# Dividing the loads of V by partitions instead of by head pairs, in a kernel of linear attention and a token-mixing MLP

## The chip, the cores and the metric

The kernel runs on one core of one Trainium2 chip. A core has TensorE (PE, with the weight loads PEld beside it), VectorE (DVE), ScalarE (ACT), GpSimd (POOL), SyncE (SP), which here issues all transfers, and 16 DMA engines. The metric is the device time of one execution in microseconds (us), of which the median over several runs is taken.

## The reference, cut to what matters

```python
# q, k, v: (8, 8, 576, 64) f32 = batch, heads, positions, head dim
c, s = cos(pi/2 * pos/S), sin(pi/2 * pos/S)
phi = lambda x: concat([relu(x)*c, relu(x)*s], -1)
kv  = einsum('bhsf,bhsd->bhfd', phi(k), v)
z   = sum(phi(k), over s)
attn = einsum('bhsf,bhfd->bhsd', phi(q), kv) / (einsum('bhsf,bhf->bhs', phi(q), z) + 1e-6)
x = attn as (8, 576, 512)
W = einsum('bsd,btd->bst', x @ w_q, x @ w_k) / 8        # w_q, w_k: (512, 64)
out = relu(einsum('bst,btd->bsd', W, x)) @ w_out        # w_out: (512, 512)
```

## The kernel before

Work is cut into 16 units, H = 0 to 15: batch H // 2, and two of its four pairs of heads. Of each of k, q and v a unit has a raw tile of 128 partitions x 2 head pairs x 576 floats (a pair's data, 2 x 576 x 64 numbers, is read as 128 rows of 576, one to a partition: a row is 2304 contiguous bytes in DRAM). There are four raw buffers for each of k, q and v (`NRAW`), taken in turn by H % 4.

The order of all work is written out by hand in ORDER (L24 to L60); a word is a step, its unit, a place in PSUM after the colon and an engine after the @ (A is ACT, V is DVE, G is POOL). Each engine does its words strictly in this order, SyncE too, which has the loads LK, LQ, LV, the weight loads LW and the stores ST in its queue. The steps that matter here:

- LV, LK, LQ (`load`, L129): a unit's raw tile comes in by two transfers of 128 partitions, one for each head pair (L132). Only for H = 0 the halves are words of their own (LV0a, LV0b and so on).
- CV (L208, cast at L193 or L195): v to bf16, over both halves, on POOL (one half on ACT). VS (L213, DVE) multiplies it by the cos and sin table.
- RK, RQ (L187 on ACT, L189 on POOL): relu of k and q to bf16.
- KV (L234): 36 matmuls of phi(k) with v; KE (L193, L197) copies the sums out of PSUM. QT (L245): transposes of q; QM (L253, DVE) multiplies by the table.
- N (L269), EP (L277, L279), X (L286, L287): numerator, denominator and their quotient, into the tile x.
- XT or XR (L300, L313) and XE: x transposed. WK (L333), WQ (L346), KX (L360), MX (L383), ME (L394, L396), WO (L403): the token mixing as (x w_k)^T x first, then times x w_q, relu, times w_out. KW, QW, XK, XA, XB are its copies between (L193, L195, L197).
- OE (L193, L197) copies an output tile of 128 rows out of PSUM, ST (L413) stores it. LW (L417 to L421) are the three weight loads.

In all SyncE issues 135 transfers: 32 for each of k, q and v, 36 stores and 3 of weights. They take eight completion semaphores in turn, and before a transfer is issued the one that had its semaphore before it, eight transfers earlier, must have landed. A load also waits until the raw buffer's last reader (RK, RQ or CV of H - 4) is done, a store until its OE is done.

Of the kernel before, what the change touches and what calls it, by code (L numbers as in the profile page):

```python
# [63 lines left out]
def kernel(  # L64
# [10 lines left out]
    nc = tc.nc  # L75
# [4 lines left out]
    P = 128  # L80
# [12 lines left out]

    NRAW, NPREP, NV2, NQM, NX, NXT, NOUT = (4, 2, 2, 2, 2, 2, 12)
    XC = DM // 2

    pool = ctx.enter_context(tc.tile_pool(name="sb", bufs=1))
    psum = ctx.enter_context(tc.tile_pool(name="ps", bufs=1, space=bass.MemoryType.PSUM))
# [2 lines left out]
    def bufs(n, shape, dtype, name):  # L101
        return [pool.tile(shape, dtype, name=f"{name}{i}") for i in range(n)]

    raw = {nm: bufs(NRAW, [P, 2, HC], FP32, f"{nm}raw") for nm in "kqv"}
# [10 lines left out]
    wq_b = bufs(2, [P, HS], BF16, "wq")  # L115
    kx_b = bufs(2, [P, 2, XC], BF16, "kx")
    mix_b = bufs(2, [P, NDM, 2 * S], BF16, "mix")
# [5 lines left out]
    def srcs(src):  # L123
        return [src[b].flatten().rearrange("(pr p e) -> p pr e", pr=NPAIR, p=P)
                for b in range(B)]

    src = {"k": srcs(k), "q": srcs(q), "v": srcs(v)}

    def load(nm, H, part):  # L129
        b, h = divmod(H, 2)  # L130
        for r in (0, 1) if part is None else (part,):
            nc.sync.dma_start(raw[nm][H % NRAW][:, r, :], src[nm][b][:, 2 * h + r, :])  # L132

# [57 lines left out]
    def cast(eng, dst, s):  # L191
        if eng is A:
            A.copy(dst, s)  # L193
        elif eng is G:
            G.tensor_scalar(dst, s, 1.0, 1.0, op0=ALU.mult, op1=ALU.mult)  # L195
        else:
            V.tensor_copy(dst, s)  # L197
# [127 lines left out]
    def bank(i):  # L325
        return PS[:, i, :].bitcast(FP32)
# [28 lines left out]
    def KX(b, ps, eng):  # L355
        place["KX", b] = ps
        o = bank(ps)
        for u in range(SC):
            for t in range(2):
                nc.tensor.matmul(  # L360
                    o[H2 * t:H2 * t + H2, 0:XC], wk_b[b % 2][:, u, :],
                    x_b[b % NX][:, u].rearrange("p h d -> p (h d)")[:, t * XC:(t + 1) * XC],
                    start=(u == 0), stop=(u == SC - 1))

    def XK(b, ps, eng):
        cast(eng, kx_b[b % 2][:, 0, :], bank(place["KX", b])[:, 0:XC])

# [66 lines left out]
    for word in ORDER.split():  # L434
        word, _, eng = word.partition("@")
        word, _, ps = word.partition(":")
        part = {"a": 0, "b": 1}.get(word[-1])
        word = word.rstrip("ab")
        kind = word[:2] if word[:2] in steps or word[0] in "LRCVT" else word[0]
        i, ps = int(word[len(kind):] or 0), int(ps or 0)  # L440
        if kind in ("LK", "LQ", "LV"):
            load(kind[1].lower(), i, part)
        elif kind in halves:
            halves[kind](i, ps, ENG.get(eng), slice(0, 2) if part is None else
                         slice(part, part + 1))
        else:
            steps[kind](i, ps, ENG.get(eng))
# [30 lines left out]
```

## Time and profile before

| what | value |
|---|---|
| three runs | 126.8, 122.39, 124.22 us; median 124.22 |
| the profiled execution | 122.49 us |
| its span, first to last instruction | 120.7 us |
| granted TensorE clock | 0.991 |
| PE, DVE, ACT, POOL busy | 94.8, 88.2, 84.2, 52.2 us |
| packets of the transfers' queue | 20592, 39.07 MB, 89.8% of 16 engines' span |
| a V load, issue to landing, median | 6.0 us |

Busy time is that of an engine's own instructions; waits, branches and the issuing of transfers are not counted. A DMA share is the sum of the packets' times over 16 engines' time; packets overlap a little in an engine, so it can be somewhat above 1. In a list of instructions in order of time a line has the start, the time from the first start to the last end of what was merged, the engine and the line of the code, the tiles, the count, and in brackets the idle time ahead of it and what ended that. SPq is SyncE issuing a transfer. The chain is followed back from the last instruction, at each step to what released it.

### The profile page before, as it was taken

The page shows a single profiled execution, that of the slowest core. Times are in us where ns is not written, and L with a number is a line of the kernel's source. Part 1 is how long each engine was busy: PE and PEld are TensorE (multiplying, and loading weights), DVE is VectorE, ACT ScalarE, POOL GpSimd, SP SyncE. Part 2 cuts the span into 40 slices and gives each one's busy share as a digit, 9 for nine tenths or more (in the row PEclk, how much of TensorE's full clock was granted, in tenths as well). Part 3 has the DMA queues.
Part 4 walks back from the last instruction along what each step waited for, and adds up shares of the span by engine and source line. Part 5 has one row for each costly group of instructions (what it writes and reads, how often), then busy time and mean ns, then how long its engine had stood idle before and what let it go on. Part 6 is the DMA issues. An engine that isn't in the chain of part 4 may idle for free.

```text
span 120.7 us, 5301 instructions
## 1 busy us (share of the span) xinstructions
PE 94.8 (79%) x2286; PEld 63.1 (52%) x2286; DVE 88.2 (73%) x132; ACT 84.2 (70%) x155; POOL 52.2 (43%) x63
## 2 busy tenths in 40 slices
PE   0005919758778899969999999798999999999950
PEld 0004818637656656635667576454755864653410
DVE  0136998889989998997979987759969868766200
ACT  7246452967887989777967897586678668757450
POOL 2577136032739758146799304937365310010000
PEclk9999999999999999999999999999999999999996
DMA  3999999999999999999989999999997681875685
GB/s 111 318 384 405 395 391 391 361 405 396 392 390 408 398 337 344 355 360 379 383 282 326 364 285 391 343 331 283 391 299 263 238 329 55 320 288 198 237 331 196
DMA packets 20615, 39.40 MB, mean 326 GB/s; under 512 B 3184, under 2 KB 3184, under 8 KB 20592
## 3 DMA queue, kind: packets, MB, share of 16 engines
q1 hardware_dynamic: 20592, 39.07, 89.8%
q8 instruction: 18, 0.29, 1.0%
q14 instruction: 5, 0.04, 0.1%
HBM read 29.62 MB, written 9.44 MB: 324 GB/s over the span
## 4 chain that ended last, share of the span: by engine, by line
DMA 39%; PE 39%; DVE 6%; issue 4%; SPq 3%; ACT 3%; POOL 2%; DVEq 0%; ACTq 0%; POOLq 0%
DMA kraw<-in_k_dram 24%; PE ps L403 20%; DMA vraw<-in_v_dram 11%; DMA out_dram<-o 5%; PE ps L234 3%; PE ps L383 3%; PE ps L269 3%; SPq L132 3%; PE ps L360 3%; DVE v L213 2%; PE ps L313 2%; DVE x L287 2%; PE ps L245 2%; PE ps L333 2%; PE ps L346 2%
## 5 line engine op out<-in xcount | busy, mean ns | idle before, releaser
L403 PE MATMUL ps<-wow,mix 128*128 128x512 bf16 x144 | 34.7, 380 | 0.0
L287 DVE TENSOR_TENSOR x<-ps,rec 128x640 bf16<-128x640 f32 x32 | 26.4, 824 | 2.2
L195 POOL TENSOR_SCALAR vb<-vraw 128x1152 bf16<-128x1152 f32 (+1 forms) x16 | 17.9, 1122 | 20.9 <-DMA vraw<-in_v_dram 18.6
L213 DVE TENSOR_TENSOR v<-vb,vtab 128x2304 bf16<-128x2304 bf16 (+1 forms) x17 | 21.7, 1289 | 6.6 <-POOL vb L195 6.6
L253 DVE TENSOR_TENSOR qm<-ps,qtab 128x2304 bf16<-128x2304 bf16 x16 | 21.4, 1350 | 4.6 <-ACT qtab L166 2.9
L193 ACT COPY o<-ps 128x512 f32<-128x512 f32 x30 | 17.5, 587 | 6.6 <-PE ps L403 4.5
L269 PE MATMUL ps<-kvs,qm 64*128 64x65 bf16 x640 | 15.3, 199 | 6.0 <-ACT kvs L193 3.3
L403 PEld LDWEIGHTS <-mix 128*128 128x128 bf16 x144 | 12.4, 98 | 14.2 <-issue 0.9
L394 ACT ACTIVATE mix<-ps 128x576 bf16<-128x576 f32 x26 | 16.4, 657 | 3.2 <-PE ps L383 3.2
L189 POOL TENSOR_SCALAR rq<-qraw 128x1152 bf16<-128x1152 f32 x9 | 13.4, 1487 | 11.4 <-DMA qraw<-in_q_dram 10.8
L269 PEld LDWEIGHTS <-qm 64*128 64x128 bf16 x640 | 13.3, 100 | 9.4 <-issue 5.7
L189 POOL TENSOR_SCALAR rk<-kraw 128x1152 bf16<-128x1152 f32 (+1 forms) x12 | 13.8, 1150 | 9.4 <-DMA kraw<-in_k_dram 7.0
L193 ACT COPY xT<-ps 128x1280 bf16<-128x1280 bf16 (+1 forms) x13 | 15.4, 1186 | 3.3 <-PE ps L313 1.7
L234 PE MATMUL ps<-v,rk 64*64 64x130 bf16 x576 | 12.5, 236 | 3.0 <-DVE x L287 1.3
L245 PE MATMUL ps<-ident,rq 64*128 64x64 bf16 x288 | 7.6, 199 | 9.3 <-ACT rq L187 8.8
L187 ACT ACTIVATE rq<-qraw 128x1152 bf16<-128x1152 f32 (+1 forms) x8 | 8.4, 1046 | 6.6 <-DMA qraw<-in_q_dram 6.6
L234 PEld LDWEIGHTS <-rk 64*64 64x64 bf16 x576 | 10.1, 117 | 5.2 <-ACT rk L187 1.4
L245 PEld LDWEIGHTS <-rq 64*128 64x128 bf16 x288 | 6.1, 101 | 11.7 <-ACT rq L187 9.0
L383 PE MATMUL ps<-wq,kx 64*128 64x288 bf16 x64 | 8.3, 287 | 0.3 <-ACT xT L193 0.2
L195 POOL TENSOR_SCALAR kx<-kx 64x256 bf16<-64x256 bf16 x7 | 2.8, 399 | 12.6 <-ACT kx L193 12.2
L286 DVE RECIPROCAL rec<-rec 128x10 f32<-128x10 f32 x32 | 6.8, 211 | 1.8 <-ACT rec L277 1.4
L277 ACT ACTIVATE rec<-ps,eps 128x10 f32<-128x10 f32 x23 | 6.2, 273 | 1.7 <-PE ps L269 1.6
(46 smaller groups left out, 99.3 us busy)
## 6 DMA issues: line engine op xcount, KB each, us to landing
vraw<-in_v_dram SPq DMA_DIRECT2D x32, 288.0 KB, 6.0
qraw<-in_q_dram SPq DMA_DIRECT2D x32, 288.0 KB, 5.9
kraw<-in_k_dram SPq DMA_DIRECT2D x32, 288.0 KB, 5.9
out_dram<-o SPq DMA_DIRECT2D x36, 256.0 KB, 3.1
wof<-in_moe_w_out_dram SPq DMA_DIRECT2D x1, 1024.0 KB, 7.6
wqf<-in_moe_w_q_dram SPq DMA_DIRECT2D x1, 128.0 KB, 5.5
wkf<-in_moe_w_k_dram SPq DMA_DIRECT2D x1, 128.0 KB, 5.2
```

What stands on the lines that cost most here:

```text
L189: eng.tensor_scalar(dst, s, FMAX, 0.0, op0=ALU.min, op1=ALU.max)
L193: A.copy(dst, s)
L195: G.tensor_scalar(dst, s, 1.0, 1.0, op0=ALU.mult, op1=ALU.mult)
L213: V.tensor_mul(v2_b[H % NV2][:, part, :, :, 0:D], vb_b[H % NPREP][:, part].unsqueeze(3).to_broadcast([P, n, C, 2, D]), vtab.unsqueeze(1).t ...
L234: nc.tensor.matmul(kv_v[o, r, :], rk_b[H % NPREP][a, pr, c, :], v2_b[H % NV2][a, pr, c, :, 0:D + 1], start=(c == 0), stop=(c == C - 1))
L245: nc.tensor.transpose(qt_v[:, r, c * H2:(c + 1) * H2], rq_b[H % NPREP][a, c, :, :], ident[a, a])
L253: V.tensor_mul(qm_b[H % NQM][:, :, :, 0:C, :].rearrange("p s r c d -> p s r (c d)"), qt_view(place["QT", H]).unsqueeze(1).to_broadcast([P, ...
L269: nc.tensor.matmul(nv[:, pr, u, :], qm_b[H % NQM][a, s, r, 2 * u:2 * u + 2, :], kv_b[H % 2][a, r, s, 0:D + 1], start=(u == 0 and s == 0), ...
L287: V.tensor_tensor(x_b[b % NX][:, :, 4 * h:4 * h + 4, :].rearrange("p u (w r) d -> p r w u d", r=2)[:, r], nv[:, :, :, 0:D], rec.to_broadca ...
L383: nc.tensor.matmul(pair(ps)[:, t, :].bitcast(FP32)[:, 0:HS], kx_b[b % 2][a, (m // 2) ^ t, (m % 2) * P:(m % 2 + 1) * P], wq_b[b % 2][a, :], ...
L394: A.activation(dst, s, AF.Relu, scale=scale_moe)
L403: nc.tensor.matmul(o, mix_b[bp % 2][:, m, rt * P:(rt + 1) * P], wow[:, m, :], start=(m == 0), stop=(m == NDM - 1))
```

## The change

A whole load of V (all but those of H = 0) still has two transfers, and they still fill the same tile from the same addresses. But the tile is divided between them by partitions: the first transfer takes the first m partitions, of both head pairs, the second one the other 128 - m. m goes through 120, 104, 88 and 72 with H % 4. K and Q are loaded as before.

```diff
     NRAW, NPREP, NV2, NQM, NX, NXT, NOUT = (4, 2, 2, 2, 2, 2, 12)
     XC = DM // 2
+    PM = (120, 104, 88, 72)
...
     def load(nm, H, part):
         b, h = divmod(H, 2)
+        if nm == "v" and part is None:
+            m = PM[H % 4]
+            for p in (slice(0, m), slice(m, P)):
+                nc.sync.dma_start(raw[nm][H % NRAW][p], src[nm][b][p, 2 * h:2 * h + 2, :])
+            return
         for r in (0, 1) if part is None else (part,):
             nc.sync.dma_start(raw[nm][H % NRAW][:, r, :], src[nm][b][:, 2 * h + r, :])
```

The lines of the code from L96 on stand one further down in the changed kernel, those from L134 on six: L195 is L201 there, L234 is L240.

## The prediction

> **What bounds the kernel now.** I read the page's forty slices first, then the busy time by stretches, SyncE's issues in order of time, the chain that ended last, and last the two engines on which the final load is used. The slices:
>
> ```profile
> PE   0005919758778899969999999798999999999950
> DMA  3999999999999999999989999999997681875685
> GB/s 111 318 384 405 395 391 391 361 405 396 392 390 408 398 337 344 355 360 379 383 282 326 364 285 391 343 331 283 391 299 263 238 329 55 320 288 198 237 331 196
> ```
>
> A slice is 3 us. The 16 DMA engines are busy from the second slice to the 30th; TensorE is full in most slices only from the 15th on. Four stretches, with the busy time of PE, PEld, DVE, ACT and POOL, the granted clock, the DMA share and GB/s:
>
> ```profile
> 3.00:33.00 30.00, 16.57 (x516) 14.45 (x517) 22.11 (x35) 17.78 (x31) 13.61 (x20) 1.00 1.05 384
> 33.00:62.00 29.00, 26.04 (x723) 17.59 (x720) 25.92 (x36) 24.29 (x49) 18.56 (x17) 1.00 1.02 370
> 62.00:92.00 30.00, 27.86 (x703) 17.88 (x696) 24.73 (x39) 22.37 (x44) 16.05 (x16) 1.00 0.98 334
> 92.00:121.00 29.00, 24.30 (x362) 13.21 (x360) 15.45 (x25) 17.47 (x33) 3.36 (x5) 0.96 0.63 235
> ```
>
> Until 33 us only the DMA is full; from 33 to 92 us DMA and TensorE are both nearly full; after 92 us the loads are over. The last row also tells what kind of limit the DMA has: at a share of 0.63 the engines move 235 GB/s, 373 for a full share, and in the first row 384/1.05 = 366. An engine does not get faster when others rest, so each has its own rate. That rate is in SyncE's issues (start, us, line, transfer):
>
> ```profile
> 12.25 1.08 SPq L132 DMA_DIRECT2D vraw<-in_v_dram  x2
> 13.76 1.08 SPq L132 DMA_DIRECT2D kraw<-in_k_dram  x2
> 15.26 1.08 SPq L132 DMA_DIRECT2D qraw<-in_q_dram  x2
> ```
>
> Here an issue waits for the landing of the transfer eight before it, so two transfers land per 1.50 us, one per 0.75. A transfer is 128 rows of 2304 bytes (576 floats), 8 for each of 16 engines: a row costs an engine 0.75/8 = 0.094 us. That each uses all 16 is in the packet counts: 3184 packets are under 512 bytes, 1024 of them rows of the two small weight loads (2 x 128 x 4), which leaves 2160 = 135 transfers x 16, one small packet for each engine of each transfer. The chain:
>
> ```profile
> 8.25 6.24 DMA vraw<-in_v_dram
> ...
> 14.51 6.51 DMA kraw<-in_k_dram
> ...
> 21.04 5.22 DMA kraw<-in_k_dram
> ...
> 26.28 6.51 DMA vraw<-in_v_dram
> ...
> 64.38 4.83 DMA kraw<-in_k_dram
> ...
> 69.22 7.16 DMA kraw<-in_k_dram
> ...
> 110.17 6.17 PE ps L403 x28
> ```
>
> One transfer releases the next until 32.8 us; the load that lands at 76.38 is on it again; the end is TensorE's. And where the last K load is used:
>
> ```profile
> 91.91 2.26 POOL L189 TENSOR_SCALAR rk<-kraw 128x1152 bf16<-128x1152 f32 x2 [2.23 <-DMA kraw<-in_k_dram]
> ```
> ```profile
> 93.69 0.75 PE L333 MATMUL ps<-wkw,xT 128*128 128x64 bf16 x20
> 94.36 1.25 PE L234 MATMUL ps<-v,rk 64*64 64x130 bf16 x72
> ```
>
> POOL idles 2.23 us for it, ends the two casts at 94.17, and TensorE starts the 72 matmuls on them at 94.36. The load stream sets the time almost to its last load.
>
> **The change, part by part.** *Removed and added.* For 15 of the 16 values of H (H = 0 is loaded in halves and stays) two V transfers of 128 rows become two of 2m and 256 - 2m rows, m = 120, 104, 88, 72. Bytes, rows of 2304, the number of transfers (135) and SyncE's order stay. Issues cost 0.33 to 0.43 us of SyncE each, at most 135 x 0.43 = 58 us of 120.7, so issue time has room; bounds for the new shapes: 0 and, at the longest step between issues inside a pair, 15 x 2 x 0.1 = 3 us, spread over a queue that waits for landings anyway. I take 0; if that cover went, it would be those 3 us at most. CV already waited for both transfers: no wait is added or removed there.
>
> *Moved: which engine carries which row.* No row of this trace shows a transfer of another count than 128, so I bound it. Lower end: 256 rows on 16 engines evenly, as now, 0 us. Upper end of an uneven spread: a transfer takes as many engines as divide its partitions into equal whole shares, always the same first ones. 128 into 16 shares of 8 is what is seen; 120, 104 and 88 give 15, 13 and 11 shares of 8, 72 gives 12 of 6; the rests give 8 of 1, 12 of 2, 10 of 4, 14 of 4. Two rows a partition, the first eight engines then carry 16+2 = 18, 16+4 = 20, 16+8 = 24 and 12+8 = 20 rows for a V load, where they carried 16; the last engine carries none. I take this end: the shares seen are equal and whole, and equal shares of 8 are what the new counts allow.
>
> [...]
>
> Extra rows on the busiest engines: H = 4, 8, 12 give 3 x 2, H = 1, 5, 9, 13 give 4 x 4, H = 2, 6, 10, 14 give 4 x 8, H = 3, 7, 11, 15 give 4 x 4: 70 rows x 0.094 = 6.6 us. By stage, in the order of the loads: 26 rows, 2.4 us, to V4, on which the chain leaves the DMA at 32.78; 48 rows, 4.5 us, to K9 (used at 58); 58 rows, 5.4 us, to K12 (landed at 76.38, used at 76.49); 70 rows, 6.6 us, to K15.
>
> *What of it is on the path.* Until 33 us all. From 33 to 62 TensorE has 3 us of idle time in 29 and waits on little, so a part is covered there; but the stretch to 92 is entered late, and K12 and K15 are used 0.11 and 0.15 us after they land. Behind a late K load on POOL, in order, stand the other casts and the small copies of L195; behind a late V or K on SyncE all later loads and stores, each waiting for the landing eight before; TensorE waits for rk at L234 with WO, MX and N queued behind. At the end the slack is small: K15's cast ends at 93.06, K14's behind it on POOL at 94.17, and the second half of the 72 matmuls starts at 94.36 + 0.6 = 95.0: 0.8 us. After that come 22 us of TensorE work in order that cannot be moved ahead. The end moves by 6.6 - 0.8 = 5.8 us.
>
> *Sum.* The profiled execution took 122.49 us, 120.7 its span and 1.8 around it. 122.49 + 5.8 = 128.3. The median of the three runs, 124.22, is 1.7 above the profiled execution; a median to be measured again has that too: 130.0 us.
>
> **The rivals.** *A: rows get slower as well.* A row costs 0.094 us when a transfer is laid out over all 128 partitions. With other shares two engines may write into the same part of the memory at a time and halve each other. Bounds for the big piece's 16 rows: unchanged, 0, or doubled, 15 x 16 x 0.094 = 22.6 us. For: 0.094 is met by all engines at once only in that one layout. Against: engines are not in step, so a clash lasts for a part of a piece. At a third to a half of the upper bound it adds 7.5 to 11.3 us: 137.5 to 141.3.
>
> [...]
>
> *B: the gaps take the rows; not slower.* Loads do not move at the full rate throughout: 384 GB/s to 33 us, 370 to 62, 334 to 92. Against the first that is 29 x 14/384 + 30 x 50/384 = 1.1 + 3.9 = 5.0 us in which the stream stands or waits for one late engine. If these gaps belong to engines that now carry less, or to SyncE waiting (11.4 us for ACT's o at L413, not all of it felt), the rows fill them: 5.8 - 5.0 = 0.8, 125.0 us. It decides only if nearly all gaps lie so; against it, gaps that come from a release which itself waits for a load move along with that load.
>
> *C: the spread is even.* Rows are dealt out evenly whatever the count, the change then does nothing to the stream: 124.2 us. Against it, only the shares above.
>
> *D: faster.* The lightly loaded engines bring their part of every Q and K earlier, but a transfer counts as landed with its slowest engine. I see no term; 122 or less.
>
> **How the numbers follow.** The forecast 0.43, A 0.28, B 0.12, C 0.13, D 0.04. The time is the forecast's, 130.0; its own range, with 4 to 7 us added, is 128.2 to 131.2. The range reaches over B to A's upper price: 125.0 to 141.5; C, D and A's upper tail, 0.2, lie outside. About 2% (121.7 to 126.7) is what a measurement of this kernel tells from no change. Same: C 0.13 and most of B, 0.09: 0.22. Slower: the forecast, A and the rest of B: 0.74. Faster: 0.04.
>
> **What the changed profile would show.** The packet counts settle the spread: by equal shares the small packets of the 15 loads fall from 32 to 23, 25, 21 and 26 each, 3 x 9 + 4 x 7 + 4 x 11 + 4 x 6 = 123 fewer, 3184 to 3061 under 512 bytes. An even spread leaves 3184. The DMA share from 3 to 33 us falls below 1.0 and GB/s by 8 to 9%; by A more. Between a V pair and the next, SyncE's issues stand more than 1.5 us apart. The last two casts of kraw on POOL start near 98.5 instead of 91.91, and the 72 matmuls of L234 near 100; the time after them is unchanged, 26 us. If the share of DMA stays at 1.05, the forecast's step on the engines is wrong; if the packets fall to 3061 and the casts still start near 92, the gaps took it; if they start after 102, rows got slower.

## The result and the profile after

The changed kernel takes 153.41 us (median of four, 150.78 to 154.61) against 124.97 before: 28.4 us more, a ratio of 1.2292, 95% interval 1.1815 to 1.2768. 130.0 was forecast, 141.5 was the upper end of the range. Some executions of every kernel fall into a slower state, so this ratio (151.56 against 123.31 us, 28.3 more) and every time, difference and ratio of the experiments below are taken from the other executions alone, while a median is over all. The profiled execution took 150.78 us, its span is 149.0. Its slices, now of 3.7 us each:

```profile
PE   0017347257984488399759998956399999999990
DMA  4999999999999998989999899998779958467785
GB/s 116 283 393 317 273 274 256 245 305 284 212 268 339 271 216 193 226 200 217 294 353 271 260 257 312 230 346 270 167 253 343 362 195 323 181 227 266 276 295 208
DMA packets 20492, 39.40 MB, mean 264 GB/s; under 512 B 3061, under 2 KB 3061, under 8 KB 20469
q1 hardware_dynamic: 20469, 39.07, 89.3%
```

Two things are to be seen. The small packets are 3061, to the packet what equal whole shares on 15, 13, 11, 12 and on 8, 12, 10, 14 engines give: in the number of engines the spread is the one that was forecast. And the DMA digits are still nines, with 200 to 350 GB/s under them where there were 340 to 400. Stretches of the changed kernel (PE, PEld, DVE, ACT, POOL, granted clock, DMA share, GB/s):

```profile
3.00:33.00 30.00, 12.19 (x356) 10.58 (x356) 16.07 (x22) 12.44 (x23) 10.78 (x17) 0.85 1.03 292
33.00:62.00 29.00, 19.35 (x424) 14.08 (x428) 20.58 (x29) 16.09 (x28) 10.46 (x11) 0.74 0.99 256
62.00:92.00 30.00, 26.52 (x606) 17.16 (x603) 19.93 (x30) 19.08 (x38) 15.30 (x13) 0.84 0.97 264
92.00:121.00 29.00, 23.76 (x553) 15.07 (x552) 18.30 (x29) 17.91 (x35) 14.13 (x12) 0.88 0.93 289
```

For a full share the first stretch moves 292/1.03 = 283 GB/s; before it was 384/1.05 = 366. The share is a sum of packet times, so packets take longer for the same bytes. The queue line says how much: 89.3% of 149.0 us are 133.1 us per engine, 89.8% of 120.7 were 108.4, so 24.7 us more packet time for each of 16 engines. Rows that are only dealt out unevenly would have left that sum as it was (e4_rows and f2_twice below show it row by row: 102.1 and 104.4 ns in the mean against 101.7). The chain, its four V loads:

```profile
9.07 8.28 DMA vraw<-in_v_dram
...
33.73 11.18 DMA vraw<-in_v_dram
...
47.93 13.73 DMA vraw<-in_v_dram
...
62.05 11.87 DMA vraw<-in_v_dram
```

A V load, 6.2 to 6.5 us on the chain before, is now 8 to 14, and the DMA holds the chain almost without a break to 74 us instead of 33 (in the kernel before two K loads are on it once more, from 64 to 76 us). SyncE's issues of the changed kernel, each pair let go by earlier landings:

```profile
12.82 1.38 SPq L135 DMA_DIRECT2D vraw<-in_v_dram  x2
15.75 1.96 SPq L138 DMA_DIRECT2D kraw<-in_k_dram  x2
17.92 1.85 SPq L138 DMA_DIRECT2D qraw<-in_q_dram  x2
```

The pairs stand 2.9 and 2.2 us apart where 1.5 was the rule. And the end, the last two casts of K on POOL:

```profile
120.41 2.58 POOL L195 TENSOR_SCALAR rk<-kraw 128x1152 bf16<-128x1152 f32 x2 [2.06 <-DMA kraw<-in_k_dram]
```

They start at 120.41, not near 98.5 as forecast; 28.6 us remain after that, as 28.8 did before. All of the loss lies ahead of these casts.

### The profile page after: what moved, and what is told of

Read it like the earlier page. It is cut to its first block, busy times and chain, and to the rows that moved or that the text cites. A ratio compares the mean times of both kernels' runs of the same rounds, so it can differ in the third digit from the quotient of the medians.

```text
span 149.0 us, 5301 instructions
## 1 busy us (share of the span) xinstructions
PE 105.9 (71%) x2286; PEld 70.0 (47%) x2286; DVE 90.2 (61%) x132; ACT 85.0 (57%) x155; POOL 54.5 (37%) x63
## 2 busy tenths in 40 slices
DMA packets 20492, 39.40 MB, mean 264 GB/s; under 512 B 3061, under 2 KB 3061, under 8 KB 20469
## 3 DMA queue, kind: packets, MB, share of 16 engines
q1 hardware_dynamic: 20469, 39.07, 89.3%
## 4 chain that ended last, share of the span: by engine, by line
DMA 51%; PE 38%; POOL 3%; SPq 3%; ACT 2%; issue 1%; ACTq 0%; POOLq 0%
DMA vraw<-in_v_dram 30%; PE ps L409 19%; DMA kraw<-in_k_dram 15%; DMA out_dram<-o 5%; PE ps L275 3%; PE ps L389 3%; PE ps L240 3%; PE ps L251 2%; PE ps L339 2%; PE ps L319 2%; PE ps L352 2%; PE ps L366 2%; POOL vb L201 2%; SPq L138 1%; SPq L135 1%
## 5 line engine op out<-in xcount | busy, mean ns | idle before, releaser
L409 PE MATMUL ps<-wow,mix 128*128 128x512 bf16 x144 | 37.5, 403 | 0.0
L201 POOL TENSOR_SCALAR vb<-vraw 128x1152 bf16<-128x1152 f32 (+1 forms) x16 | 18.4, 1153 | 45.1 <-DMA vraw<-in_v_dram 44.1
L275 PE MATMUL ps<-kvs,qm 64*128 64x65 bf16 x640 | 15.7, 203 | 11.5 <-DVE qm L259 5.3
L240 PE MATMUL ps<-v,rk 64*64 64x130 bf16 x576 | 14.7, 261 | 9.7 <-POOL rk L195 4.4
L400 ACT ACTIVATE mix<-ps 128x576 bf16<-128x576 f32 x26 | 16.3, 654 | 8.6 <-PE ps L389 8.6
L195 POOL TENSOR_SCALAR rk<-kraw 128x1152 bf16<-128x1152 f32 (+1 forms) x12 | 14.6, 1217 | 11.4 <-DMA kraw<-in_k_dram 8.0
L240 PEld LDWEIGHTS <-rk 64*64 64x64 bf16 x576 | 12.0, 134 | 12.3 <-POOL rk L195 5.4
L251 PE MATMUL ps<-ident,rq 64*128 64x64 bf16 x288 | 9.0, 215 | 11.6 <-ACT rq L193 10.6
L195 POOL TENSOR_SCALAR rq<-qraw 128x1152 bf16<-128x1152 f32 x9 | 13.1, 1460 | 9.1 <-DMA qraw<-in_q_dram 8.1
L251 PEld LDWEIGHTS <-rq 64*128 64x128 bf16 x288 | 7.2, 110 | 16.7 <-ACT rq L193 10.7
L389 PE MATMUL ps<-wq,kx 64*128 64x288 bf16 x64 | 9.5, 310 | 3.5 <-ACT o L199 2.3
L193 ACT ACTIVATE rk<-kraw 128x1152 bf16<-128x1152 f32 (+1 forms) x5 | 5.3, 1067 | 8.6 <-DMA kraw<-in_k_dram 5.8
L201 POOL TENSOR_SCALAR kx<-kx 64x256 bf16<-64x256 bf16 x7 | 4.0, 567 | 12.5 <-ACT kx L199 12.1
L199 ACT CAST kvs<-ps 128x260 bf16<-128x260 f32 x12 | 4.5, 381 | 7.0 <-PE ps L240 7.0
```

The costliest lines, as they stand in the source:

```text
L195: eng.tensor_scalar(dst, s, FMAX, 0.0, op0=ALU.min, op1=ALU.max)
L240: nc.tensor.matmul(kv_v[o, r, :], rk_b[H % NPREP][a, pr, c, :], v2_b[H % NV2][a, pr, c, :, 0:D + 1], start=(c == 0), stop=(c == C - 1))
L251: nc.tensor.transpose(qt_v[:, r, c * H2:(c + 1) * H2], rq_b[H % NPREP][a, c, :, :], ident[a, a])
L275: nc.tensor.matmul(nv[:, pr, u, :], qm_b[H % NQM][a, s, r, 2 * u:2 * u + 2, :], kv_b[H % 2][a, r, s, 0:D + 1], start=(u == 0 and s == 0), ...
L389: nc.tensor.matmul(pair(ps)[:, t, :].bitcast(FP32)[:, 0:HS], kx_b[b % 2][a, (m // 2) ^ t, (m % 2) * P:(m % 2 + 1) * P], wq_b[b % 2][a, :], ...
L400: A.activation(dst, s, AF.Relu, scale=scale_moe)
```

## The experiments

Theory I: only the uneven counts of rows per engine cost. Theory S: rows get slower because engines write into the same part of the memory. Theory N: the order in which DRAM is read, or two head pairs in one transfer, is slow. Theory C, from the g runs on, is a form of S: how crowded the fullest part of the memory is in a transfer decides. S and C are suppositions of the author: no trace names the engine of a packet or the part of the memory that it writes, only times can speak for them. Times are means; in brackets is the difference to the mean of the kernel before, measured on the same chip beside it (122.85 for the e runs, 123.16 for f, 122.78 for g, 123.78 for h, 122.44 for i), then the ratio with its 95% interval. e2_64, e3_96, g_120, g_88 and h2_near rest on one execution each and h4_pairs on two, so they have no interval. The expectations were written from medians (12.1 us for f2_twice, for example), which differ by up to 4 us.

**e1_whole.**
```diff
-            for p in (slice(0, m), slice(m, P)): ...
+            nc.sync.dma_start(raw[nm][H % NRAW], src[nm][b][:, 2 * h:2 * h + 2, :])
```


> Each whole V load is one transfer of 128 partitions with both head pairs, so the rows of the two pairs alternate as in the changed kernel, but the partitions are dealt out as before the change. Theory S (rows got slower because engines that share a piece write into the same part of the memory) and theory I (only the uneven counts of rows per engine): both expect no loss, 122 to 126 us. Theory N (the alternating order of the rows in DRAM, or rows of two pairs in one transfer, is what is slow): 140 to 153 us.

126.85 us (+4.0; ratio 1.0325, 1.0176 to 1.0475). N falls: reading two pairs in turn costs a few us at most, not 28. The few were not followed up.

**e2_64 and e3_96.** m = 64, and m = 96, for every H.

> Each whole V load is divided 64 + 64: if the number of engines is the largest up to 16 that divides the partitions, every engine has 8 rows of each transfer, as before the change, and under 512 bytes stay 3184 packets. Theory I: no loss, 122 to 127 us. [...] Theory N: 140 to 153 us.

> Each whole V load is divided 96 + 32, again 16 engines and even counts, 12 + 4 rows for each. Theory I: no loss, 122 to 127 us. Theory S: the 4 rows of the piece of 32 cost up to double, 15 x 4 x 0.094 = 5.6 us, the 12 of the piece of 96 anything from nothing to double, 16.9 us: 129 to 147 us. Theory N: 140 to 153 us.

143.67 us (+20.8) and 140.05 (+17.2). By equal shares nothing is uneven here (both have 3184 small packets, as before the change) and most of the loss is there: I cannot be the main cause. e3_96 is in S's range, and +20.8 for e2_64 is near the 15 x 16 x 0.094 = 22.6 us that doubled rows of V would cost.

**e4_rows, f2_twice.** The loads of before, and a further transfer (two in f2_twice) for each whole V load:
```diff
+            n = (2, 4, 8, 4)[H % 4]
+            nc.sync.dma_start(scr[H % 4:32:4, 0:n, :], vrows[b][n][0:8])
```


> The loads are those before the change; beside each whole V load stands a third transfer of 2, 4, 8 or 4 further rows (with H % 4) for each of 8 engines, into an unused tile, on partitions 0, 4, 8 to 28 (shifted by H % 4), which are taken to be those that the same 8 engines write anyway: the uneven counts of the forecast (70 rows more on the busiest engines) without any sharing. 1.3 MB more are loaded. The forecast's own price, 70 x 0.094 = 6.6 less 0.8: theory I and theory S as the larger of two parts both expect 128 to 132 us. If 124 to 126, the gaps took the rows and the loss of the change is all from slower rows; if above 134, uneven counts cost more than the rows that they add.

> e4_rows with the extra rows twice (two transfers for each V load, 140 rows more on the busiest engines, again every fourth partition). It prices the forecast's step by itself: 140 x 0.094 = 13.2 less 0.8 gives 12.4 us over the kernel before, 134 to 139 us. If the gaps in the stream take the rows (rival B), 126 to 130 us.

126.86 us (+4.0; ratio 1.0326, 1.0182 to 1.0469, where 5.8 us would be 1.047) and 136.80 (+13.6; 1.1096, 1.0977 to 1.1216). Twice the rows cost about what 140 x 0.094 - 0.8 = 12.4 said. The single dose lies under its price; some rows may be taken by gaps, but the doubled dose excludes that gaps swallow them all. 4 to 7 us, from the single dose to half of the double one, is a fair price for the change's 70 rows. It includes whatever the 15 or 30 further transfers cost in themselves.

**f1_near, f4_pairs.** e4_rows with other partitions, meant for the same 8 engines:
```diff
-            nc.sync.dma_start(scr[H % 4:32:4, 0:n, :], vrows[b][n][0:8])
+            nc.sync.dma_start(scr[8 * (H % 4):8 * (H % 4) + 8, 0:n, :], vrows[b][n][0:8])  # f1_near
+            nc.sync.dma_start(scr[H % 4:64:8, 0:n, :], vrows[b][n][0:8])                   # f4_pairs
```


> As e4_rows, the same 70 extra rows on the same 8 engines in the same transfers, but written to 8 neighbouring partitions (8 x (H % 4) and the 7 after it) in place of every fourth. Theory I (only the count of rows per engine matters): as e4_rows, 126 to 129 us. Theory S (engines that write into the same part of the memory halve each other): if 4 engines share each of two such parts, a row costs up to 4 x 0.094, 70 x 0.38 = 26.3 less 0.8: 135 to 151 us.

> [...] Theory I: 126 to 129 us. Theory S: a row up to double, 70 x 0.188 = 13.2 less 0.8, so between e4_rows and 138 us, and below f1_near.

138.15 us (+15.0; 1.1217, 1.1130 to 1.1304) and 132.28 (+9.1; 1.0740, 1.0543 to 1.0938). Same bytes, same source rows and the same number of engines as e4_rows' +4.0 (3304 small packets in all three, 8 for each further transfer); only the partitions written differ. That the eight engines are the same ones is assumed, no count shows it. The order, neighbours worst (+15.0), then every eighth (+9.1), then every fourth (+4.0), is the one in which theory S had priced them.

**f3_evenodd.** e2_64 with `(slice(0, P, 2), slice(1, P, 2))`.

> V divided 64 + 64 as in e2_64, but into even and odd partitions, so that each transfer reaches all of the memory and each engine has the same 8 rows of it. Theory I: as before the change, 123 to 127 us. Theory S as the number of parts reached (64 neighbours reach half of them): 123 to 128 us. [...]

124.71 us (+1.6; 1.0126, 1.0049 to 1.0203). Its stretches:

```profile
3.00:33.00 30.00, 15.91 (x508) 13.97 (x508) 21.02 (x34) 16.90 (x29) 13.70 (x19) 1.00 1.04 379
33.00:62.00 29.00, 26.38 (x716) 17.92 (x710) 27.27 (x35) 24.91 (x50) 18.15 (x17) 1.00 1.01 368
62.00:92.00 30.00, 26.90 (x668) 17.33 (x660) 24.87 (x40) 21.86 (x44) 16.56 (x16) 1.00 0.93 324
```

379/1.04 = 364 GB/s for a full share, the rate of before. Dividing V by partitions costs almost nothing if the partitions are chosen so. It seemed to speak for theory C, and the next four put that to the test.

**g_120, g_88, g_112.** m = 120, 88, 112 for every H. **g_big.** The piece of 120 alone:
```diff
+        if nm == "v" and H >= NRAW:
+            nc.sync.dma_start(raw[nm][H % NRAW][0:120], src[nm][b][0:120, 2 * h:2 * h + 2, :])
```


> The change with m = 120 for every H. Uneven counts alone (theory I, priced by f2_twice at 12.1 us for 140 rows): 15 x 2 = 30 rows, 2.6 us: 127 to 129 us. [...] Theory S (engines in step halve each other also in the piece of 120): up to 22.6 more: 145 to 150 us.

> The change with m = 88 for every H. Theory I: 15 x 8 = 120 rows, 10.4 us: 134 to 137 us. [...] Theory S: 22.6 + 10.4 = 33: 153 to 158 us.

> For H >= 4 only the piece of 120 partitions of V is loaded, the piece of 8 is left out (the last 8 partitions keep the rows of an earlier H, so the output is another); H = 1 to 3 are loaded by head pairs. 15 engines have 16 rows as before, the last has none. Theories I and C: as the kernel before, 122 to 126 us. Theory S: the piece of 120 by itself costs up to double, 12 x 16 x 0.094 = 18 us: 134 to 143 us.

> V divided 112 + 16: by the counts all 16 engines take part in both pieces, 14 + 2 rows each, nothing is uneven. Theory I: 123 to 126 us. [...]

143.36 us (+20.6), 155.07 (+32.3), 140.27 (+17.5; 1.1429, 1.1217 to 1.1642) and 143.87 (+21.1; 1.1722, 1.1529 to 1.1915). Theory C falls with g_big, for which it expected no loss: by equal shares no engine has more rows than before, the small piece is not there, and yet 12 such loads cost 17.5 of the 12 x 16 x 0.094 = 18 us that doubled rows would. g_112 has all 16 engines in each transfer, by equal shares evenly loaded (its small packets are 3184), and loses as much:

```profile
DMA packets 20615, 39.40 MB, mean 276 GB/s; under 512 B 3184, under 2 KB 3184, under 8 KB 20592
```
```profile
3.00:33.00 30.00, 12.72 (x356) 10.90 (x356) 16.08 (x23) 11.87 (x23) 10.90 (x17) 0.97 1.02 299
```

The first line is g_112's packets, their counts as before the change; the second its first stretch, 293 GB/s for a full share. In g_120 and g_88 both causes act, and they lie on either side of the change (+20.6 and +32.3 against its 28.3). g_88 is g_112's 21.1 and 120 x 0.094 - 0.8 = 10.5 for its rows, to within 1 us.

**h1_wide, h2_near.** Source and destination of e2_64 and f3_evenodd crossed:
```diff
+            for p, w in zip((slice(0, P, 2), slice(1, P, 2)), (slice(0, H2), slice(H2, P))):   # h2_near: the two swapped
+                nc.sync.dma_start(raw[nm][H % NRAW][p], src[nm][b][w, 2 * h:2 * h + 2, :])
```


> The DRAM side of e2_64 (first 64 rows of both pairs, then the other 64) with the memory side of f3_evenodd (even, then odd partitions); rows of V land on other partitions than they should, so the output is another. If the place of writing decides: as f3_evenodd, 122 to 127 us. If the order of reading decides: as e2_64, 142 to 149 us.

> The other way round: DRAM side of f3_evenodd (even rows, then odd ones), memory side of e2_64 (64 neighbouring partitions, then the other 64); V is permuted here too. If the place of writing decides: 142 to 149 us. If the order of reading decides: 122 to 127 us.

124.60 us (+0.8; 1.0059, 0.9991 to 1.0126) and 143.59 (+19.8). The place of writing decides, the order of reading does not: written to alternate partitions V costs 0.8 and 1.6 us more than before (h1_wide, f3_evenodd), written to 64 neighbours 19.8 and 20.8 (h2_near, e2_64), in either order of reading.

**h3_60, h4_pairs, i2_48.** g_big's loads (H >= 4, the rest left out) over other partitions or by pairs:
```diff
+            for p in (slice(0, 120, 2), slice(1, 120, 2)): ...        # h3_60; i2_48: 96 in place of 120
+            for r in (0, 1): ... raw[nm][H % NRAW][0:120, r, :] ...   # h4_pairs
```


> g_big's 120 partitions of V (H >= 4, the last 8 partitions left out) in two transfers of 60, even and odd partitions: 15 engines, 4 partitions each, 8 apart in all as in g_big. If every second partition is what spares f3_evenodd: 122 to 127 us. If 16 engines in place of 15 is what spares it: as g_big, 138 to 143 us.

> g_big's 120 neighbouring partitions (H >= 4, the last 8 left out) in two transfers by head pairs, as the kernel before loads its 128: 15 engines, 8 neighbouring partitions each, but 4 rows in turn on four neighbouring partitions in place of 8. If the length of such a run decides (engines wait out a short clash with what they have in flight): 122 to 128 us. If neighbouring partitions in equal shares do: as g_big, 138 to 143 us.

> As h3_60 with 96 of the partitions: two transfers of 48, even and odd, for H >= 4 (the last 32 partitions left out), which 16 engines share by 3; a quarter less of V is loaded. If 16 engines are what spares f3_evenodd: 116 to 125 us. If only the count of 64 (or 128) is dealt out so that each engine writes at home: slower than the kernel before, 127 to 138 us.

138.41 us (+14.6; 1.1165, 1.1030 to 1.1301), 134.53 (+10.8) and 131.14 (+8.7; 1.0714, 1.0361 to 1.1068). Every second partition does not spare 60 or 48, nor does a count that 16 divides (48), nor, for 120 neighbours, the division by head pairs (h4_pairs), though each of these loses less than g_big. i2_48 loads a quarter less of V for H >= 4 and is still slower than the whole.

**i1_far.** f2_twice with `for p in (64, 96)` in place of `(0, 32)`.

> [...] If only sharing inside a transfer costs: as f2_twice, 135 to 138 us. If writing where another engine is at home costs: up to double for the extra rows, 138 to 150 us.

144.37 us (+21.9; 1.1791, 1.1594 to 1.1988) against f2_twice's +13.6. The further rows and the transfers are the same in number, only the half of the partitions is another, and the loss is 8.3 us larger. The author had taken partitions 64 to 127 for those that other engines write in the ordinary loads; if so, it is the cost of writing there. No trace shows that they are.

```profile
3.00:33.00 30.00, 11.72 (x352) 10.37 (x353) 15.00 (x21) 11.47 (x22) 10.91 (x17) 0.93 0.96 304
```
```profile
3.00:33.00 30.00, 13.62 (x418) 12.01 (x420) 18.24 (x27) 14.04 (x26) 10.92 (x17) 0.89 0.97 342
```

The first stretch of i1_far above, of f2_twice below: 317 and 353 GB/s for a full share, from the partition numbers alone.

**The rows themselves.** The traces have the time of every packet, and each row of 2304 bytes is one packet: 12288 of them in the kernel before, 96 transfers of q, k and v x 128. The mean time of such a packet, and the share of them that took over 150 ns, for thirteen of the kernels:

| run | mean, ns | over 150 ns |
|---|---|---|
| before | 101.7 | 2.7% |
| e1_whole | 100.1 | 2.2% |
| f3_evenodd | 101.4 | 2.7% |
| e4_rows | 102.1 | 3.0% |
| f2_twice | 104.4 | 4.0% |
| f4_pairs | 109.1 | 8.2% |
| i1_far | 114.6 | 16.5% |
| f1_near | 115.2 | 10.7% |
| i2_48 | 116.9 | 14.1% |
| h4_pairs | 119.0 | 16.3% |
| h3_60 | 120.6 | 18.7% |
| g_112 | 130.1 | 31.6% |
| the change | 132.6 | 32.5% |

Further rows for eight engines (e4_rows, f2_twice) leave the time of a row almost as it was; the place of writing changes it. In the changed kernel a row takes 30.9 ns more in the mean, 12288/16 x 30.9 = 23.7 us for each engine, nearly all of the 24.7 above. In the kernel before 96.7% of the rows took 110 ns or less, although half of all rows go to partitions 64 to 127, so this half is not slow in itself. And i1_far has 1666 more packets over 150 ns than f2_twice, which is more than its 1120 far rows: ordinary rows are slowed too.

## Why the prediction was wrong, point by point

*What bounds the kernel* held in the main: the load stream sets the time to its last load, and the last loads are used as soon as they land. After the last K casts the end keeps its distance (28.6 and 28.8 us). Where the loss arises can be read at the KV matmuls: those of unit 4 start at 49.46 in place of 37.94 us (11.5 late), of unit 8 at 80.83 in place of 58.06 (22.8 late), of unit 11 at 95.11 in place of 71.50 (23.6), and the last ones at 123.14 in place of 94.36 (28.8). So four fifths of it are there by unit 8, while the DMA holds the chain; from unit 8 to 11 the chain is TensorE's and hardly anything is added.

*Which engine carries which row* held to the packet in the number of engines: 3061 small packets in the changed kernel, 123 fewer than before, and in g_120 3049, 9 fewer for each of 15 loads, as 15 + 8 engines in place of 32 give. That they are always the same first engines no count shows; that f2_twice costs the full price of 140 rows on one engine (13.6 us against 12.4) speaks for it.

*70 rows x 0.094 = 6.6, less 0.8* was about the right price of that step: e4_rows gives 4.0 us, f2_twice 13.6 for twice as many.

*The step that failed* is the price of a row. "a row costs an engine 0.75/8 = 0.094 us" was taken from transfers of 128 partitions and applied to rows of the new pieces too. That rows get slower was left to rival A, at a third to a half of its bound of 22.6 us, because "engines are not in step, so a clash lasts for a part of a piece". The runs show nearly the whole bound: 28.3 less the 4 to 7 for uneven counts leaves 21 to 24; the packets are 23.7 us longer per engine; g_112 gives 21.1 with nothing uneven by equal shares, g_big 17.5 of 18. The engines are out of step: the 16 completions of a load, in the trace of the kernel before, lie 2.1 us apart from first to last (median of 96 loads). That did not spare the rows. Why not was not shown; the author supposes that nearly every engine of the piece writes where some other engine is at work on this or the next transfer. The forecast thus had the smaller of two parts, and A's chance, 0.28, and its price were both too low.

*Rival A's mechanism*, two engines that halve each other inside a piece, was not shown, and it is too narrow: f3_evenodd spares the rows (+1.6 us), h3_60 does not (+14.6), and i1_far loses 8.3 us more than f2_twice through the other half of the partitions alone. The author's wider supposition, that in a transfer of 128 partitions or of 64 alternate ones each engine writes where no other one does, and in the other pieces tried not, fits all eighteen runs, up to the few us of e1_whole; by it the places in e4_rows and f2_twice were chosen. It was not shown: no trace here names the engine of a packet, so that engines meet at a place, and which partitions an engine gets in any of these transfers, stays open. What is shown is that the place of writing decides how long a row takes: 102.1, 109.1 and 115.2 ns in e4_rows, f4_pairs and f1_near, 104.4 and 114.6 in f2_twice and i1_far, each with the same rows.

*Rivals B, C, D* of the prediction: the gaps do not take 140 rows (f2_twice); the even spread (rival C, not theory C) is excluded by the packet counts; nothing got faster.

*One reading rule of the prediction misled.* It said that the DMA share would fall below 1.0 and that a share still at 1.05 would refute the step on the engines. The share stayed at 1.03 although some engines carry less, because it adds up the times of packets, and these grew for the same bytes. The packet counts and GB/s per share were the sure signs. The rule "if they start after 102, rows got slower" (120.41) was right.

Left open: the 4.0 us of e1_whole; and how much the lower granted clock adds (0.74 in the second stretch, where TensorE waits for loads and the chain is the DMA's). After that it has little room: from unit 8 to unit 12 (80.83 to 103.31 us) the clock is 0.98, and from there to the last KV, at 0.83, TensorE is busy 17.39 us with the work that took 15.60 at 1.00, so 1.8 us at most come from it there.

## What to carry to other kernels

The price of a transfer's row is only known for the layout in which it was measured; when an edit changes the partitions of a transfer, price the place of writing before the count of rows, and measure a row in the new layout by itself (101.7 ns before, 132.6 in the change). Full use of 16 engines is not enough: 112 + 16, 96 + 32 and 64 + 64 all use 16 by their packet counts (3184) and cost 17 to 21 us here, alternate 64s 1.6. And read a DMA share together with GB/s: the same nines stood over 384 and over 292.

## What the runs showed of the hardware that was not expected

Where a row is written can more than double what it costs, with bytes, source and number of engines unchanged (e4_rows +4.0, f4_pairs +9.1, f1_near +15.0 us for the same 70 rows per engine). A division into 64 even and 64 odd partitions is almost free (+1.6 us), one into 60 and 60 is not (+14.6, on less data).
